# Attention and a gated product on one core: 128 partitions as two heads times 64 token groups, with the array used in tiles

## The chip, the cores and the metric

The kernel runs on one core of one Trainium2 chip. The metric is the device time of the launch in microseconds, lower is better. Times "before" are 292.38 and 290.5 us, median 291.44 us.

## The reference

For 8 batches and 8 heads of 576 tokens by 64 channels, q is put through a softmax over its channels, k through a softmax over the tokens. `kv` is the 64x64 product of the two token axes of k and v, and each token's output is its softmaxed q times `kv`. The result, as 4608 tokens by 512 channels (x), goes through a gated product and two matrices:

```
q_s = exp(q) / sum over channels         k_s = exp(k) / sum over tokens
kv = einsum('bhsd,bhse->bhde', k_s, v)   x = einsum('bhsd,bhde->bhse', q_s, kv)
a = x @ w1 ; b = x @ w2                  # w1, w2: 512 x 1024
out = ((a * b) @ w3) @ w_out             # w3: 1024 x 1024, w_out: 1024 x 512
```

The kernel folds w3 @ w_out into one 1024x512 matrix, W3O, once. All inputs and the output are float32, and the kernel computes in float16 with float32 sums.

## The kernel before, in words

One batch of 8 heads is the unit of the attention, one chunk of 512 tokens (of 9) the unit of what follows. A batch is 576 tokens, so chunk j needs batches up to j.

The attention of a batch has an elementwise part and a matrix part. A load (`load_qkv`) brings q, k or v of four heads; 96 partitions hold 6 tokens each (R = 6), so one row of a partition is 6 x 64 floats, 1536 bytes. `exp_k` and `exp_q` run on ScalarE (ACT) for a pair of heads at a time, `cast_v` on GpSimd (POOL) for four heads, and `norm_q` sums on VectorE (DVE), takes the reciprocal there, and multiplies on GpSimd. The matrix part is cut into pieces, which `pieces(b)` lists: `piece_t` transposes the normed q of a pair of heads (6 transposes into PSUM and one DVE copy to `qsT`), `piece_kv` accumulates `kv` of two pairs (12 matmuls; a column of 1/32 in v gives the sum of exp(k), so that DVE divides on the way to `kv2`), and `piece_x` multiplies `qsT` by a block-diagonal `kv2` (2 matmuls of 288 columns for a pair) and ScalarE copies the result into `xT`.

A chunk has 8 groups `s1` (four matmuls to `pa`, which ScalarE copies to float16; four to `pb`, which DVE multiplies with that copy) and, one chunk later, 4 groups `s2` (eight matmuls with W3O; DVE scales, and SyncE issues two stores of the rows). `w3_t` and `w3_m` make W3O: eight transposes of a row block of w3, then eight matmuls with w_out.

The order of the work is written out by hand: every engine runs its instructions in the order of the program. It is: loads and elementwise part of batch 0, its pieces, `s1` of chunk 0, the W3O loop (with the exps of the first half of batch 1 put in at `ft == 5`), then the four `s2` of chunk 0 between the pieces of batch 1, then the whole elementwise part of batch 2. From chunk 1 on, a table `seq` of 12 steps runs: each step has one `s1` or `s2`, then one piece of batch j+1, then one elementwise step of batch j+2, then perhaps a load of batch j+3. All loads and stores are issued by SyncE (SP), in program order. Every load goes into one of 9 slots of the pool `stage`, and waits until its slot is free. PSUM has three buffers for the attention (`pAtt`), three for `s1` (`pAB`) and two for `s2` and W3O (`pO`).

Of the kernel before, what the change touches and what calls it, by code (L numbers as in the profile page):

```python
# [16 lines left out]
def kernel(  # L17
# [11 lines left out]
    nc = tc.nc  # L29
# [4 lines left out]
    R = 6  # L34
    SP = S // R
    NPAIR = H // 2
# [9 lines left out]
    stage = ctx.enter_context(tc.tile_pool(name="stage", bufs=9))  # L46
    attn = ctx.enter_context(tc.tile_pool(name="attn", bufs=8))
# [4 lines left out]
    xT = [konst.tile([P, T], F16, name=f"xT{i}") for i in range(N_CT)]  # L52
    v16buf = [konst.tile([SP, H, R, 66], F16, name=f"v16_{i}") for i in range(2)]
    kv2buf = [konst.tile([P, 2, P], F16, name=f"kv2_{i}") for i in range(4)]
# [5 lines left out]
    def pAtt(shape, dtype):  # L60
        return psum.tile(shape, dtype, tag="att", name="att", bufs=3)
# [4 lines left out]
    def pO():  # L66
        return psum.tile([P, C], F32, tag="po", name="po", bufs=2)
# [7 lines left out]
    def load_qkv(b, which, hf):  # L75
        src = {"q": q, "k": k, "v": v}[which]
        t = slot([SP, 4, R * D])
        nc.sync.dma_start(  # L78
            out=t, in_=src[b, 4 * hf:4 * hf + 4].rearrange("h (p r) d -> p h (r d)", r=R))
        qkv32[(which, b, hf)] = t  # L80
# [22 lines left out]
    eks = {}  # L103
    eqs = {}
    eqns = {}

    def exp_k(b, p):
        t = qkv32[("k", b, p // 2)]
        ek = attn.tile([SP, R, 2, D], F16, tag="ek", name="ek", bufs=8)
        o = 2 * (p % 2)  # L110
        nc.scalar.activation(  # L111
            out=ek.rearrange("p r h d -> p h r d"),
            in_=t[:, o:o + 2].rearrange("p h (r d) -> p h r d", r=R), func=AF.Exp)
        eks[(b, p)] = ek

    def exp_q(b, p):
        t = qkv32[("q", b, p // 2)]
        eq = attn.tile([SP, R, 2, D], F16, tag="eq", name="eq", bufs=4)
        o = 2 * (p % 2)
        nc.scalar.activation(  # L120
            out=eq.rearrange("p r h d -> p h r d"),
            in_=t[:, o:o + 2].rearrange("p h (r d) -> p h r d", r=R), func=AF.Exp)
        eqs[(b, p)] = eq

    def cast_v(b, hf):
        t = qkv32[("v", b, hf)]
        nc.gpsimd.tensor_copy(  # L127
            out=v16buf[b % 2][:, 4 * hf:4 * hf + 4, :, 0:D],
            in_=t.rearrange("p h (r d) -> p h r d", r=R))

    def norm_q(b, p):
# [259 lines left out]
```

## Time and profile before

| | before |
|---|---|
| median of two runs | 291.44 us (290.5 and 292.38) |
| the profiled execution: time, span | 292.19 us, 290.4 us |
| mean granted TensorE clock | 0.964 |
| busy: PE, DVE, ACT, POOL | 245.5, 140.0, 124.3, 79.2 us |
| read and written in HBM | 38.80 MB, 9.44 MB |

The span runs from the first to the last instruction of the profiled execution; 1.8 us of its time lie outside the span. PE is TensorE's matmuls, PEld its weight loads, which run beside them. In rows of the timeline stand the start, the duration, the engine, the line of the kernel, the operation, what it writes and reads, shape and count, and in brackets the idle time before it and what ended that. A line with a form such as `96*128` names rows and columns of the array in use.

### The profile page before, as it was taken

What the parts mean: (1) busy time and instruction counts of PE and PEld (TensorE: products, weight loads), DVE (VectorE), ACT (ScalarE), POOL (GpSimd) and SP (SyncE); (2) the same over time, 40 slices, a digit from 0 to 9 for tenths busy, and PEclk for the clock granted to TensorE, in tenths of its full rate; (3) what the DMA queues carried; (4) which work ended last, traced back from release to release, by engine and by line L of the source; (5) the groups of instructions that cost most, each with busy time, mean ns of one, the idle gap of its engine ahead of it and who ended that gap; (6) DMA issues with size and microseconds to landing.
All of it is one profiled execution on the core that took longest, in us unless ns stands there. A gap on an engine that the chain in (4) does not pass through costs nothing.

```text
span 290.4 us, 3985 instructions
## 1 busy us (share of the span) xinstructions
PE 245.5 (85%) x1440; PEld 125.1 (43%) x1440; DVE 140.0 (48%) x268; ACT 124.3 (43%) x217; POOL 79.2 (27%) x64
## 2 busy tenths in 40 slices
PE   0218997739693399999999999999999999999993
PEld 0115444415441155555555455455555544444441
DVE  0344453231733468476476476657745434333441
ACT  3426542263344558556464456445622332121200
POOL 1461702305503456354125405505400000000000
PEclk9999999998888579999999999999999999999999
DMA  7999999990139999949946965971121112121124
GB/s 182 254 326 391 357 351 282 261 250 15 41 97 236 256 256 256 228 118 220 280 129 156 257 149 128 261 208 38 48 62 38 36 47 64 36 73 38 55 76 121
DMA packets 31443, 48.49 MB, mean 167 GB/s; under 512 B 2240, under 2 KB 24768, under 8 KB 31424
## 3 DMA queue, kind: packets, MB, share of 16 engines
q1 hardware_dynamic: 31424, 48.24, 62.3%
q8 instruction: 11, 0.18, 0.3%
q14 instruction: 8, 0.07, 0.1%
HBM read 38.80 MB, written 9.44 MB: 166 GB/s over the span
## 4 chain that ended last, share of the span: by engine, by line
PE 79%; DMA 8%; ACT 5%; DVE 3%; issue 1%; SPq 1%; DVEq 0%; ACTq 0%
PE pab L204 22%; PE pab L198 21%; PE po L215 21%; DMA st<-in_q_dram 8%; PE po L243 5%; PE att L152 4%; PE att L180 3%; PE att L169 2%; ACT eq L120 2%; ACT ek L111 1%; PE att L235 1%; DVE ds L134 1%; SPq L78 1%; DVE osb L218 0%; ACT w_542 L232 0%
## 5 line engine op out<-in xcount | busy, mean ns | idle before, releaser
L138 POOL TENSOR_TENSOR eqn<-eq,dr 96x768 f16<-96x768 f16 x32 | 46.8, 1470 | 98.9 <-DVE dr L136 57.5
L134 DVE TENSOR_REDUCE ds<-eq 96x12 f32<-96x768 f16 x32 | 30.0, 936 | 44.2 <-ACT eq L120 44.1
L215 PEld LDWEIGHTS <-abT 128*128 128x128 f16 x288 | 27.6, 99 | 30.5 <-issue 1.1
L218 DVE TENSOR_SCALAR osb<-po 128x512 f32<-128x512 f32 x36 | 24.8, 688 | 27.2 <-PE po L215 26.2
L120 ACT ACTIVATE eq<-st 96x768 f16<-96x768 f32 x32 | 26.4, 843 | 11.8 <-DMA st<-in_q_dram 11.8
L111 ACT ACTIVATE ek<-st 96x768 f16<-96x768 f32 x32 | 25.8, 843 | 8.5 <-DMA st<-in_k_dram 8.5
L169 PE MATMUL att<-ident,eqn 96*128 96x96 f16 x192 | 14.8, 219 | 7.7 <-POOL eqn L138 7.7
L152 PEld LDWEIGHTS <-ek 96*128 96x128 f16 x192 | 14.5, 108 | 13.9 <-ACT ek L111 7.0
L169 PEld LDWEIGHTS <-eqn 96*128 96x128 f16 x192 | 12.4, 105 | 13.9 <-POOL eqn L138 8.7
L152 PE MATMUL att<-v_0_75,ek 96*128 96x130 f16 x96 | 8.8, 254 | 10.0 <-POOL v_0_75 L127 10.0
L172 DVE COPY qsT<-att 128x576 f16<-128x576 f16 x32 | 14.2, 450 | 0.7 <-PE att L169 0.6
L204 PEld LDWEIGHTS <-w_0_85 128*128 128x128 f16 x72 | 7.4, 103 | 16.0 <-issue 8.6
L127 POOL CAST v_0_75<-st 96x1536 f16<-96x1536 f32 x8 | 11.7, 1461 | 9.2 <-DMA st<-in_v_dram 8.8
L215 PE MATMUL po<-W3O_93,abT 128*128 128x512 f16 x36 | 13.9, 386 | 0.0
L215 PE MATMUL po<-W3O_96,abT 128*128 128x512 f16 x36 | 13.9, 386 | 0.0
L215 PE MATMUL po<-W3O_95,abT 128*128 128x512 f16 x36 | 13.9, 385 | 0.0
L215 PE MATMUL po<-W3O_94,abT 128*128 128x512 f16 x36 | 13.9, 385 | 0.0
L215 PE MATMUL po<-W3O_97,abT 128*128 128x512 f16 x36 | 13.7, 381 | 0.0
L215 PE MATMUL po<-W3O_98,abT 128*128 128x512 f16 x36 | 13.6, 379 | 0.0
L215 PE MATMUL po<-W3O_99,abT 128*128 128x512 f16 x36 | 13.6, 379 | 0.0
L215 PE MATMUL po<-W3O_100,abT 128*128 128x512 f16 x36 | 13.6, 379 | 0.0
L204 PE MATMUL pab<-xT_71,w_0_85 128*128 128x512 f16 x18 | 7.3, 404 | 5.9 <-ACT a_880 L201 5.9
(265 smaller groups left out, 507.3 us busy)
## 6 DMA issues: line engine op xcount, KB each, us to landing
st<-in_k_dram SPq DMA_DIRECT2D x16, 576.0 KB, 9.7
st<-in_v_dram SPq DMA_DIRECT2D x16, 576.0 KB, 8.5
st<-in_q_dram SPq DMA_DIRECT2D x16, 576.0 KB, 10.0
st<-in_moe_w_dram SPq DMA_DIRECT2D x16, 512.0 KB, 7.7
out_dram<-osb SPq DMA_DIRECT2D x24, 192.0 KB, 2.3
out_dram<-osb SPq DMA_DIRECT2D x24, 128.0 KB, 2.3
st<-in_moe_w_out_dram SPq DMA_DIRECT2D x4, 512.0 KB, 5.5
out_dram<-osb SPq DMA_DIRECT2D x24, 64.0 KB, 2.0
```

The lines of the kernel that those rows point to most:

```text
L111: nc.scalar.activation(out=ek.rearrange("p r h d -> p h r d"), in_=t[:, o:o + 2].rearrange("p h (r d) -> p h r d", r=R), func=AF.Exp)
L120: nc.scalar.activation(out=eq.rearrange("p r h d -> p h r d"), in_=t[:, o:o + 2].rearrange("p h (r d) -> p h r d", r=R), func=AF.Exp)
L134: nc.vector.tensor_reduce(out=ds, in_=eq, axis=AX.X, op=ALU.add)
L138: nc.gpsimd.tensor_tensor(out=eqn.rearrange("p r h d -> p (r h) d"), in0=eq, in1=dr[:, :, None].broadcast_to([SP, 2 * R, D]), op=ALU.mult)
L152: nc.tensor.matmul(kvp[:, pp, :].rearrange("p (h e) -> p h e", h=2), lhsT=ek[:, r].rearrange("p h d -> p (h d)"), rhs=v16buf[b % 2][:, 2 * ...
L169: nc.tensor.transpose(pt[:, r, :], eqn[:, r].rearrange("p h d -> p (h d)"), ident[:SP, :SP])
L172: nc.vector.tensor_copy(out=qsT, in_=pt.rearrange("p r s -> p (r s)"))
L198: nc.tensor.matmul(pa, lhsT=w1sb[qt][:, ct, fo:fo + P], rhs=xT[ct][:, t0:t0 + CH], start=(ct == 0), stop=(ct == N_CT - 1))
L204: nc.tensor.matmul(pb, lhsT=w2sb[qt][:, ct, fo:fo + P], rhs=xT[ct][:, t0:t0 + CH], start=(ct == 0), stop=(ct == N_CT - 1))
L215: nc.tensor.matmul(po, lhsT=abT[(j, ft)][:, tb * P:(tb + 1) * P], rhs=W3O[ft], start=(ft == 0), stop=(ft == N_FT - 1))
L218: nc.vector.tensor_scalar(out=osb, in0=po, scalar1=ISC, scalar2=None, op0=ALU.mult)
L243: nc.tensor.matmul(wps, lhsT=w3Ts[ft][:, gt, :], rhs=wosb[gt // 2][:, gt % 2, :], start=(gt == 0), stop=(gt == N_FT - 1))
```

## The change

R becomes 9: a partition now holds 9 tokens of one head (2304 bytes in a row), 64 partitions hold a head, and 128 partitions hold two adjacent heads, g = 0 and 1. A load brings two such couples of heads (index hh), so it still covers four heads, and a half i of a batch is one such load of q, k and v. Elementwise instructions have 576 elements in each partition (one couple), or 1152 (two couples, in `norm_q`).

- `piece_kv(b, i)`: for each of 9 token rows two matmuls of 64 array rows, g = 0 and g = 1, into two PSUM banks; 18 matmuls, and two pieces in a batch.
- `piece_t(b, i)`: 9 transposes of 128x128 in place of 6 of 96x96; two in a batch, not four.
- `piece_x(b, i, hf)`: four matmuls of 64x64 array tiles (two row halves hh, two column halves g), 288 columns each; four pieces in a batch, and one ScalarE copy of 576 elements for each. `kv2` is no longer block-diagonal.
- `stage` has 12 slots, `pAtt` 2 buffers of two banks, `pO` one buffer; the last `s2` of the program and those of chunk 0 use `pAtt` in turn (`alt`).
- Order: q first in batch 0; w1 and w2 before w_out; two blocks of w3 ahead of w_out; all of w3 ahead of batch 1. Two `w3_t` stand within `s1` of chunk 0, and the W3O loop runs two blocks ahead. All casts of w3 are on GpSimd. Batch 1's exps begin after the seventh `w3_m`. The six loads of batch 2 are issued after the second `s2` of chunk 0, those of batch 3 after the fourth. In batch 0, v is cast by DVE and ACT, and the second half of q is multiplied by DVE.

```diff
-    R = 6
+    R = 9
-    stage = ctx.enter_context(tc.tile_pool(name="stage", bufs=9))
+    stage = ctx.enter_context(tc.tile_pool(name="stage", bufs=12))
...
+            in_=src[b, 4 * i:4 * i + 4].rearrange("(h g) (s r) d -> (g s) h (r d)", g=2, r=R))
...
+    def piece_kv(b, i):
+        kvp = pAtt([P, 2, 512], F32)
+        for r in range(R):
+            for g in range(2):
+                rows = slice(64 * g, 64 * g + 64)
+                nc.tensor.matmul(kvp[:, g, 0:130].rearrange("p (h e) -> p h e", h=2),
+                                 lhsT=eks[(b, i)][rows, r].rearrange("p h d -> p (h d)"),
+                                 rhs=v16buf[b % 2][rows, 2 * i:2 * i + 2, r, 0:65],
                                  start=(r == 0), stop=(r == R - 1))
...
+        for hh in range(2):
+            rows = slice(64 * hh, 64 * hh + 64)
+            for g in range(2):
+                nc.tensor.matmul(xp[64 * g:64 * g + 64, hh, 0:HS], lhsT=kv2[rows, g, :],
+                                 rhs=qsT[rows, g, cols], start=True, stop=True)
+        nc.scalar.copy(out=xT[:, 2 * i:2 * i + 2, b * S + hf * HS:b * S + (hf + 1) * HS],
+                       in_=xp[:, :, 0:HS])
...
-        (nc.scalar.copy if ft % 2 else nc.gpsimd.tensor_copy)(out=w316, in_=w32[("3", ft)])
+        nc.gpsimd.tensor_copy(out=w316, in_=w32[("3", ft)])
...
-        wps = pO()
+        wps = pO() if ft % 2 else pAB()
...
     for ft in range(N_FT):
-        if ft + 1 < N_FT:
-            w3_t(ft + 1)
         w3_m(ft)
-        if ft == 3:
-            for which in "kvq":
-                load_qkv(1, which, 1)
-        if ft == 5:
-            load_qkv(2, "k", 0)
-            elementwise(1, 0)
-    load_qkv(2, "v", 0)
-    load_qkv(2, "q", 0)
-    elementwise(1, 1)
+        if ft + 2 < N_FT:
+            w3_t(ft + 2)
+        if ft >= 6:
+            ew[2 * (ft - 6)]()
+            ew[2 * (ft - 6) + 1]()
...
+        s2(0, tb, alt=tb % 2)
+        ew[4 + tb]()
...
+        if tb == 1:
+            pc[1]()
+            for i in range(2):
+                load_qkv(2, "q", i)
+                load_qkv(2, "k", i)
+                load_qkv(2, "v", i)
```

Where the instructions moved, as the built programs have them. First ScalarE in the W3O loop, before; `w_` is a cast of a block of w3, `W3O` the copy of a finished block, `ek` and `eq` the exps of batch 1:

```order
L245 CAST W3O_96<-po 128x512
L232 CAST w_542<-st 128x1024
L245 CAST W3O_97<-po 128x512
L245 CAST W3O_98<-po 128x512
L111 ACTIVATE ek<-st 96x2x6x64 x2
L120 ACTIVATE eq<-st 96x2x6x64 x2
L232 CAST w_611<-st 128x1024
L245 CAST W3O_99<-po 128x512
```

And ScalarE at the same place now:

```order
L240 CAST W3O_91<-po 128x512
L240 CAST W3O_92<-pab 128x512
L114 ACTIVATE eq<-st 128x9x64 x2
L240 CAST W3O_93<-po 128x512
L107 ACTIVATE ek<-st 128x9x64 x2
L114 ACTIVATE eq<-st 128x9x64 x2
```

No cast of w3 stands on ScalarE any more, and no exp stands ahead of one. Second SyncE around the first stores, before; the three loads ahead of the stores are the first half of batch 2, those behind them its second half:

```order
L78 DMA st<-in_k_dram 96x4x384
L78 DMA st<-in_v_dram 96x4x384
L78 DMA st<-in_q_dram 96x4x384
L224 DMA out_dram<-osb 96x512
L224 DMA out_dram<-osb 32x512
L224 DMA out_dram<-osb 64x512 x2
L224 DMA out_dram<-osb 32x512
L224 DMA out_dram<-osb 96x512 x2
L224 DMA out_dram<-osb 32x512
L78 DMA st<-in_k_dram 96x4x384
```

And SyncE there now; the loads ahead of the stores are the second half of batch 1, the six between the stores are batch 2:

```order
L76 DMA st<-in_v_dram 128x2x576
L220 DMA out_dram<-osb 64x512 x4
L76 DMA st<-in_q_dram 128x2x576
L76 DMA st<-in_k_dram 128x2x576
L76 DMA st<-in_v_dram 128x2x576
L76 DMA st<-in_q_dram 128x2x576
L76 DMA st<-in_k_dram 128x2x576
L76 DMA st<-in_v_dram 128x2x576
L220 DMA out_dram<-osb 64x512 x4
```

Of batch 2, no load stands ahead of the stores now; all six stand behind four of the eight.

More of the change, by code (lines that the diff above doesn't have):

```diff
@@ L100, in load_w3 @@
         w32[("3", ft)] = t
[L103 to L123, printed above, removed]
@@ L245, in w3_m @@
         nc.scalar.copy(out=W3O[ft], in_=wps)
[L248 to L257 removed]
+    ctx.enter_context(tc.manual_schedule())
+    acopy, vcopy, pcopy = nc.scalar.copy, nc.vector.tensor_copy, nc.gpsimd.tensor_copy
+    for i in range(2):
+        for which in "qkv":
+            load_qkv(0, which, i)
     load_w12(0, 0)
```

288 lines of the change are left out of this document (150 added, 138 removed).

## The prediction

> **What bounds the kernel now.** I read the page's 40 slices first. A slice is 7.26 us; each digit is a busy share in tenths.
>
> ```profile
> span 290.4 us, 3985 instructions
> PE   0218997739693399999999999999999999999993
> DMA  7999999990139999949946965971121112121124
> ```
>
> From the fifteenth slice (about 102 us) on, PE is full to the last slice but one. All idle time that a change of order could take away lies before it, and there the DMA row is full until 65 us. So there are two questions: how much earlier the full stretch starts, and whether a chunk in it gets shorter. For the first I read the timeline of PE and ACT at each gap:
>
> ```profile
> 6.09 1.58 ACT L111 ACTIVATE ek<-st 96x768 f16<-96x768 f32 x2 [4.06 <-DMA st<-in_k_dram]
> 8.46 1.46 POOL L127 CAST v_0_75<-st 96x1536 f16<-96x1536 f32 x1 [6.67 <-DMA st<-in_v_dram]
> 9.97 1.46 PE L152 MATMUL att<-v_0_75,ek 96*128 96x130 f16 x12 [9.97 <-POOL v_0_75 L127]
> 10.75 1.58 ACT L120 ACTIVATE eq<-st 96x768 f16<-96x768 f32 x2 [3.08 <-DMA st<-in_q_dram]
> 27.21 0.63 PE L198 MATMUL pab<-xT_71,w_0_81 128*128 128x512 f16 x1
> 42.58 0.61 PE L235 MATMUL att<-ident,w_431 128*128 128x128 f16 x8
> 49.89 0.62 PE L235 MATMUL att<-ident,w_490 128*128 128x128 f16 x8 [1.62 <-ACT w_490 L232]
> 65.10 1.03 PE L235 MATMUL att<-ident,w_611 128*128 128x128 f16 x8 [4.55 <-ACT w_611 L232]
> 70.36 0.38 PE L215 MATMUL po<-W3O_93,abT 128*128 128x512 f16 x1
> 85.48 0.38 PE L198 MATMUL pab<-xT_71,w_0_81 128*128 128x512 f16 x1
> 97.20 1.58 ACT L120 ACTIVATE eq<-st 96x768 f16<-96x768 f32 x2 [3.07 <-DMA st<-in_q_dram]
> 99.29 0.58 PE L204 MATMUL pab<-xT_71,w_0_85 128*128 128x512 f16 x1 [5.88 <-ACT a_880 L201]
> ```
>
> These rows cut the start into five stages: batch 0's attention until 27.21, `s1` of chunk 0 until 42.58, the W3O loop until 70.36, batch 1 with `s2` of chunk 0 until 85.48, and a stall in the second group of chunk 1 until 99.29. In the third, PE waits for casts of w3 on ACT; the longest wait, 4.55 us, is for the cast that stands behind batch 1's exps. In the fifth, the copy `a_880` stands on ACT behind batch 2's exps, and those wait for loads.
>
> For the second question, the fourth `s2` of three chunks in the chain of waits:
>
> ```profile
> 211.64 1.73 PE po L215 x8
> 235.78 1.73 PE po L215 x8
> 256.50 1.73 PE po L215 x8
> ```
>
> A chunk with a batch's pieces takes 24.14 us (211.64 to 235.78), one without 20.72: the pieces cost PE 3.42 us a batch, on the path, six times (batches 2 to 7).
>
> **The loads.** The windows show what the loads get (the last two columns are DMA share and GB/s):
>
> ```profile
> 4.00:17.70 13.70, 2.78 (x24) 2.19 (x24) 2.21 (x4) 4.74 (x7) 5.77 (x4) 1.00 1.08 252
> 17.70:40.00 22.30, 17.47 (x85) 8.61 (x86) 11.98 (x24) 11.56 (x20) 8.30 (x7) 1.00 1.01 362
> 88.00:106.00 18.00, 8.74 (x42) 4.45 (x43) 8.11 (x16) 8.12 (x12) 8.67 (x6) 0.62 1.06 256
> ```
>
> The first and the third are loads of q, k and v into 96 partitions, the second is weights into 128; the engines are full in all. One load of 589.8 KB at 252 takes 2.33 us, at 362 it takes 1.63. The new load is 128 partitions with rows of 2304 bytes. I take 1.63, since the row with 128 partitions is the nearest, and keep 2.33 as the other end. The Trainium skill ("SBUF — State Buffer", Door 1: the DMA port swizzle) has 16 ports of 8 partitions, by which 96 partitions fill half of the ports only half; it would give 252/0.75 = 336 GB/s, an estimate, 1.76 us a load and about 1 us on the sum below.
>
> **The elementwise work** shrinks by a quarter per batch, since 128 partitions share it. Groups that I scale by elements:
>
> ```profile
> L138 POOL TENSOR_TENSOR eqn<-eq,dr 96x768 f16<-96x768 f16 x32 | 46.8, 1470 | 98.9 <-DVE dr L136 57.5 <-ACT xT_71 L182 37.1 <-PE pab L198 2.6
> L134 DVE TENSOR_REDUCE ds<-eq 96x12 f32<-96x768 f16 x32 | 30.0, 936 | 44.2 <-ACT eq L120 44.1
> L120 ACT ACTIVATE eq<-st 96x768 f16<-96x768 f32 x32 | 26.4, 843 | 11.8 <-DMA st<-in_q_dram 11.8
> L232 POOL CAST w_467<-st 128x1024 f16<-128x1024 f32 x1 | 1.0, 1043 | 7.5 <-PE att L235 7.5
> L201 ACT CAST a_346<-pab 128x512 f16<-128x512 f32 x1 | 0.6, 586 | 1.1 <-PE pab L198 1.1
> L161 DVE TENSOR_TENSOR kv_0_77<-att,rc 64x128 f16<-64x128 f32 x8 | 2.3, 289 | 0.2
> L172 DVE COPY qsT<-att 128x576 f16<-128x576 f16 x32 | 14.2, 450 | 0.7 <-PE att L169 0.6
> L237 DVE COPY w3T<-att 128x1024 f16<-128x1024 f16 x8 | 5.5, 690 | 11.6 <-PE att L235 11.6
> ```
>
> An exp of 576 elements: 843 x 0.75, about 0.65 us. A sum: 0.70. A multiply of 1152 on POOL: 1.5 x 1.47 = 2.2. A copy of 1152 to `qsT`: by 450 at 576 and 690 at 1024, 0.76. A copy of x, 576 elements on ACT: by 586 at 512, 0.65. The division after `kv`: two of 0.29 and the reciprocal, about 0.75. In the full stretch PE is the bound and not these engines, so the quarter is worth nothing there; in the first stages it shortens the chain.
>
> **The stages.** *Batch 0.* Before, k's first exp starts at 6.09 and q's, two loads later, at 10.75, so a load takes 2.33 and the first began near 3.8. With 1.63 each and q first, the first lands near 5.4, the rest at 7.0, 8.7, 10.3, 11.9, 13.5. The chain then is DVE's: v cast until 9.5 (0.4 an instruction, by the 690 for 1024), nine passes of two `kv` matmuls to 10.6 (0.12 a pass, by the 12 in 1.46 at this place, where PE is slower than later), division, transposes to 11.7, `qsT` to 12.5, the two sums of the second half to 13.9, reciprocal and its multiply on DVE (1.2 ns an element, by the sum's 936 for 768) to 15.5, transposes to 16.6, `kv` to 17.7, division to 18.5, two x pieces and two copies to 20.2. Before: 27.21. Gain 7.0.
>
> *`s1` of chunk 0* takes 15.4 before (27.21 to 42.58) and gets two `w3_t` of 0.45 more: loss 0.9, end at 36.5. Its weights land in time: six loads to 13.5, then eight of 524 KB at 1.45 to 25.1; two of w3 and four of w_out by 33.8, and the last of the four is cast near 36.
>
> *W3O loop.* The cost of its parts, two rows of the timeline back to back and one of the chain of waits:
>
> ```profile
> 45.93 0.61 PE L235 MATMUL att<-ident,w_467 128*128 128x128 f16 x8
> 46.38 0.59 PE L243 MATMUL po<-wo_89,w3T 128*128 128x512 f16 x2
> 46.54 1.74 PE po L243 x8
> ```
>
> Eight transposes take 46.38 - 45.93 = 0.45 us, eight matmuls 1.74. Now 8 x 1.74 + 6 x 0.45 = 16.6, in place of 27.8 (42.58 to 70.36), if nothing waits: the casts are on POOL (1.04 us each, one for each 2.19 us), run two blocks ahead, and the last block of w3 lands near 42.5, while its transposes stand near 49. Gain 11.2; end at 53.1. If a wait of one cast stayed in every second block, as the 1.62 us above, it would be 6 less.
>
> *Batch 1 and `s2` of chunk 0.* Before 15.1 (70.36 to 85.48). Now four `s2` of 1.73 with a wait of 1.5 in them for the first multiply on POOL (exps from 51.8, two sums and the reciprocal to 54.1, multiply to 56.3), and 1.2 of pieces between them, end at 62.7. Behind the fourth, with two `pAtt` buffers, the rest goes in turn: transposes, scaling and copy to `qsT` (0.69 and 0.76), `kv` 0.53, division 0.75, two x pieces and copies 1.5, with the transposes 4.8. End at 67.5: gain 0.7. The loads of batch 2 stand on SP behind four stores, which need the second `s2`, finished near 58.6; they are issued near 60 and land from 64.8 on (4.6 after the issue, by the first load above with 1.63), the fifth (the last k) near 71.3.
>
> *The stall.* ACT has eight exps of 0.65 from 67.5, until 72.7 with no load late; then `a16` of the first group to 73.3, and the second group's `pb` goes on near 74.3. Before, the same instruction started at 99.29, 13.8 after the first `s1`; now 6.8 after. Gain 7.0. DMA is about 1 us from being late here.
>
> Sum of the five: 7.0 - 0.9 + 11.2 + 0.7 + 7.0 = 25.0 us earlier. I summed without hand-overs; one takes 0.05 (the v cast ends at 9.92, the matmul that waits starts at 9.97), some thirty in these chains, 1.5. So 23.5. Batch 3's loads follow behind batch 2's, every 1.63 us, ahead of their exps at a step of 2 us each.
>
> **The pieces in the full stretch.** What one takes now, from start to the start of the next kind:
>
> ```profile
> 142.50 0.42 PE L169 MATMUL att<-ident,eqn 96*128 96x96 f16 x6
> 142.75 0.38 PE L198 MATMUL pab<-xT_71,w_0_81 128*128 128x512 f16 x1
> 144.48 0.86 PE L152 MATMUL att<-v_0_75,ek 96*128 96x130 f16 x12
> 145.19 0.38 PE L215 MATMUL po<-W3O_93,abT 128*128 128x512 f16 x1
> 145.41 0.38 PE L215 MATMUL po<-W3O_94,abT 128*128 128x512 f16 x1
> 82.35 0.41 PE L180 MATMUL att<-qsT,kv_2_79 128*128 128x288 f16 x2
> 82.60 0.42 PE L169 MATMUL att<-ident,eqn 96*128 96x96 f16 x6
> ```
>
> Transposes of 96 columns are 42 ns each, matmuls of 130 columns 59, of 288 columns 125: 24 x 42 + 24 x 59 + 8 x 125 = 3.42 us, which is the difference of the chunks. Now 18 transposes of 128 columns (0.45/8 = 56 ns) are 1.01. The 36 `kv` matmuls are 18 x 59 = 1.06 if the two row halves run at once, 36 x 59 = 2.12 if not. The 16 matmuls of x are 4 x 125 = 0.50 if four tiles run at once, 2.0 if not. So 2.57 or 5.13 a batch, -0.85 or +1.71.
>
> No row of before shows the array changing its tiling. The nearest is the tail of a matmul that does not wait for the one before: a 512-column matmul has a record of 0.38 us and the next starts 0.216 later (145.19, 145.41), so up to 0.164 could show each time the array has to empty. A batch has two `kv` pieces and four x pieces between others: 12 changes, at most 2.0 us; at least nothing, if the next weights come in meanwhile. I take half, 0.98, with overlapping tiles: 2.57 + 0.98 = 3.55, +0.13 a batch, +0.8 in all. The Trainium skill ("TensorEngine Tiling (Array Packing)", Key Properties) says that a change of tiling mode drains the array, and that tiles run independently; by that the whole tail is paid, and that is the first rival.
>
> **Sum.** 292.2 (the profiled execution, 0.75 above the median) - 23.5 + 0.8 = 269.5. I write 270.
>
> **The rivals.** *Every change empties the array, tiles overlap.* 2.57 + 1.97 = 4.54 a batch, +1.12, six times 6.7: 275.4. For it: six pieces in a batch stand between full-size work. Against: no row; weight loads run ahead now (PEld beside PE).
>
> *Loads stay at 252 GB/s.* The bound is then the row size or HBM and not the partitions. Batch 0 loses 2 (its last v lands at 17.7), the W3O loop 1 (w_out lands 4 later), the stall 3 (the fifth load 9.3 after the first, not 6.5), batch 3's first exp 2: 8 in all, 277. Against: at 1 KB rows the weights had 362.
>
> *The start gives less.* The stall in chunk 1 stays as long as before (of batch 2, nothing is issued ahead of the stores now): 7 less, 276.5.
>
> *Tiles take turns, changes are cheap.* +1.71 seven times (batch 1 too) is 12.0, and batch 0's chain, with twice the `kv` passes at 0.12 (2.2) and x in turns (1.5), 3.7: 284.4, at the edge of what 2% can tell.
>
> *Slower: tiles take turns and every change also shows a weight load.* 5.13 + 12 x (0.164 + 0.10) = 8.30 a batch, +4.9; seven batches 34.2, batch 0 3.7: 292.2 - 23.5 + 37.9 = 306.6. The change turns against itself from (23.5 - 3.7)/7 = 2.8 us more a batch on, 6.2 in place of 3.42. The 0.10 is a weight load, as this row has it:
>
> ```profile
> L215 PEld LDWEIGHTS <-abT 128*128 128x128 f16 x288 | 27.6, 99 | 30.5 <-issue 1.1
> ```
>
> For it: 70 weight loads a batch in place of 56, on half-size tiles. Against: the 96-column transposes already go at 42 ns each with one load per matmul.
>
> **How the numbers follow.** Chances: forecast 0.45 (its own range 264, no cost of changes, to 275); every change empties 0.18; loads slow 0.10; start gives less 0.11; take turns 0.10; slower 0.06. The range 261 to 285 holds the first five nearly whole; its low end lets the start come 2.5 us earlier than summed. Two runs of before differ by 0.6%, so 2% is what can be told from no change: below 285.6 is faster. The first four are, and half of the fifth; with two in a hundred off for mishaps, faster 0.87, same 0.07, slower 0.06.
>
> **What would show it.** `s1` of chunk 0 starts near 20 to 21 and the W3O loop near 37; no wait on a cast of w3; the second group of chunk 1 goes on near 75; loads of q, k, v run at 360 GB/s. In the full stretch the fourth `s2` of two chunks stand 24.3 apart: 23.3 means free changes, 25.3 the drained array, 25.9 and more tiles that take turns. I would be wrong if that distance passes 27, or if PE's full stretch still starts after 90.

## The result and the profile after

The changed kernel takes 272.8 us (median of 272.52 and 273.09), before 291.44: a ratio of 0.936, with a 95% interval of 0.922 to 0.950. Run once more beside other versions it took 271.75 us, ratio 0.932 (0.928 to 0.936). The profiled execution took 272.52 us, its span is 270.7. The forecast for it was 269.5, so the sum was 3.0 us short.

The page of the kernel after, its 40 slices of 6.77 us each:

```profile
span 270.7 us, 4110 instructions
PE   0459999986779999999999999999999999999982
DMA  7999999118999604883495469212211113112235
```

PE is now busy from the fourth slice on, with one dip to 6 and 7 tenths in slices ten to twelve, where before it came down to 3 tenths in three slices and was full only from the fifteenth on. The DMA row is no longer full to the end of the start: it has two holes, at 47 to 61 us and at 95 to 102.

The timeline of the kernel after, at the ends of the five stages and at what they wait for:

```profile
4.49 1.26 ACT L114 ACTIVATE eq<-st 128x576 f16<-128x576 f32 x2 [2.48 <-DMA st<-in_q_dram]
19.63 2.00 PE L197 MATMUL pab<-xT,w_0_74 128*128 128x512 f16 x4
24.95 1.06 PE L203 MATMUL pab<-xT,w_0_78 128*128 128x512 f16 x4
37.11 0.59 PE L238 MATMUL pab<-wo_82,w3T 128*128 128x512 f16 x2
54.44 0.38 PE L214 MATMUL po<-W3O_86,abT 128*128 128x512 f16 x1 [0.67 <-ACT W3O_93 L240]
63.00 0.75 DVE L127 TENSOR_REDUCE ds<-eq 128x9 f32<-128x576 f16 x1
66.38 0.68 PE L165 MATMUL att<-ident,eqn 128*128 128x128 f16 x9 [2.06 <-POOL eqn L134]
70.22 2.11 PE L197 MATMUL pab<-xT,w_0_74 128*128 128x512 f16 x4
73.82 2.12 POOL L134 TENSOR_TENSOR eqn<-eq,dr 128x1152 f16<-128x1152 f16 x1 [6.28 <-DVE dr L132]
75.99 0.98 PE L165 MATMUL att<-ident,eqn 128*128 128x128 f16 x9 [2.50 <-POOL eqn L134]
76.76 1.91 PE L197 MATMUL pab<-xT,w_0_74 128*128 128x512 f16 x4
78.47 1.06 PE L203 MATMUL pab<-xT,w_0_78 128*128 128x512 f16 x2
```

The stages of the sum, in us: before and after from the starts of these instructions, the forecast from its own terms, where 75.8 is the forecast's 74.3 with the 1.5 of hand-overs put in, and 191.9 is the 191.1 of before with the 0.8 of the pieces:

| | before | forecast | after |
|---|---|---|---|
| batch 0's attention, until `s1` starts | 27.21 | 20.2 | 19.63 |
| `s1` of chunk 0 | 15.37 | 16.3 | 17.48 |
| W3O loop | 27.78 | 16.6 | 17.33 |
| batch 1 and `s2` of chunk 0 | 15.12 | 14.4 | 15.78 |
| stall, until `pb` of the second group | 13.81 | 6.8 | 8.25 |
| hand-overs, charged in one sum | | 1.5 | in the stages |
| `pb` of the second group starts at | 99.29 | 75.8 | 78.47 |
| from there to the end of the span | 191.1 | 191.9 | 192.2 |

So the start became 20.8 us shorter and the rest 1.1 us longer. The gain is batch 0 (7.6), the W3O loop (10.45) and the stall (5.6); the two stages between them became longer by 2.1 and 0.7.

The kernel after was profiled once more in its later run (270.29 us, span 268.5). In the order of the table its stages are 19.72, 16.03, 17.33, 16.25, 7.15 and 192.0. So two executions of one kernel differ by up to 1.5 us in a stage: by 1.45 in `s1` of chunk 0, 0.5 in batch 1 and 1.1 in the stall. A difference of that size between forecast and measurement says nothing about the change to the kernel.

Two windows of the kernel after, the first loads and `s1` of chunk 0; the last three columns are the granted clock, the DMA share and GB/s:

```profile
3.00:13.00 10.00, 2.62 (x35) 2.11 (x35) 5.01 (x10) 3.77 (x6) 2.12 (x1) 1.00 1.02 373
19.63:37.11 17.48, 17.48 (x81) 7.59 (x82) 7.78 (x12) 9.30 (x14) 8.52 (x8) 1.00 1.05 388
```

The loads have 373 GB/s with engines as full as they were at 252. The lengths that the forecast had scaled from the smaller tiles hold: the multiply on POOL was put at 2.2 us and is 2.12, the sum at 0.70 and is 0.75 (the rows at 73.82 and 63.00 above).

The chain of waits after, the fourth `s2` of the same three chunks:

```profile
190.38 1.73 PE po L214 x8
214.98 1.73 PE po L214 x8
235.70 1.73 PE po L214 x8
```

A chunk with pieces now takes 24.60 us, before 24.14; one without, 20.72 as before. The pieces cost PE 3.88 us a batch and not 3.42. The timeline of PE around one piece of `kv` and one of x in the full stretch shows of what these consist:

```profile
145.83 1.03 PE L203 MATMUL pab<-xT,w_0_78 128*128 128x512 f16 x4
146.79 0.69 PE L148 MATMUL att<-v_1_73,ek 64*128 64x130 f16 x18
147.42 0.39 PE L214 MATMUL po<-W3O_86,abT 128*128 128x512 f16 x1
149.15 0.67 PE L165 MATMUL att<-ident,eqn 128*128 128x128 f16 x9
149.66 1.03 PE L197 MATMUL pab<-xT,w_1_75 128*128 128x512 f16 x4
150.52 1.03 PE L203 MATMUL pab<-xT,w_1_79 128*128 128x512 f16 x4
151.48 0.32 PE L179 MATMUL att<-qsT,kv_1749 64*64 64x288 f16 x4
151.72 1.04 PE L197 MATMUL pab<-xT,w_1_75 128*128 128x512 f16 x4
```

Four matmuls of 512 columns take 0.86 from start to start (149.66 to 150.52). What follows the four at 145.83 comes after 0.96, and so it does at 150.52: 0.10 us lie in front of each piece in a new tiling. The 18 `kv` matmuls take 0.63, the four of x 0.24, the nine transposes 0.51, which are in full-size tiling. With two, four and two pieces: 2 x 0.73 + 4 x 0.34 + 2 x 0.51 = 3.84, against the 3.88 of the chunks. Overlapping tiles without a price for changes would be 2.57, as forecast; the 1.3 above it are twelve changes of 0.11. Six of them are the gaps in front of the pieces; the other six, back to full-size tiling, lie within the 0.63 and the 0.24.

### The profile page after: what moved, and what is told of

Its sections match the earlier page's. It is cut to its first block, busy times and chain, and to the rows that moved or that the text cites. A ratio compares the mean times of both kernels' runs of the same rounds, so it can differ in the third digit from the quotient of the medians.

```text
span 270.7 us, 4110 instructions
## 1 busy us (share of the span) xinstructions
PE 244.1 (90%) x1552; PEld 114.0 (42%) x1552; DVE 134.3 (50%) x236; ACT 108.1 (40%) x182; POOL 62.6 (23%) x63
## 4 chain that ended last, share of the span: by engine, by line
PE 87%; DVE 5%; POOL 2%; DMA 2%; ACT 1%; issue 1%; SPq 0%; POOLq 0%; DVEq 0%; ACTq 0%
PE pab L197 24%; PE pab L203 23%; PE po L214 20%; PE att L148 4%; PE att L165 4%; PE att L179 3%; PE pab L238 3%; POOL eqn L134 2%; DMA st<-in_v_dram 2%; PE att L214 2%; PE po L238 2%; DVE ds L127 2%; PE att L230 1%; DVE osb L217 1%; ACT xT L181 1%
## 5 line engine op out<-in xcount | busy, mean ns | idle before, releaser
L134 POOL TENSOR_TENSOR eqn<-eq,dr 128x1152 f16<-128x1152 f16 x15 | 31.8, 2121 | 99.7 <-PE att L179 48.6
L181 ACT CAST xT<-att 128x576 f16<-128x576 f32 x32 | 20.1, 639 | 37.4 <-PE att L179 37.4
L127 DVE TENSOR_REDUCE ds<-eq 128x9 f32<-128x576 f16 x32 | 23.6, 750 | 10.7 <-ACT eq L114 10.3
L114 ACT ACTIVATE eq<-st 128x576 f16<-128x576 f32 x32 | 21.3, 685 | 5.9 <-DMA st<-in_q_dram 5.9
L197 PE MATMUL pab<-xT,w_0_74 128*128 128x512 f16 x72 | 22.2, 433 | 0.1
L107 ACT ACTIVATE ek<-st 128x576 f16<-128x576 f32 x32 | 21.3, 682 | 0.2 <-DMA st<-in_k_dram 0.2
L203 PE MATMUL pab<-xT,w_0_78 128*128 128x512 f16 x72 | 20.3, 408 | 0.0
L165 PE MATMUL att<-ident,eqn 128*128 128x128 f16 x144 | 11.9, 234 | 8.1 <-POOL eqn L134 5.6
L197 PE MATMUL pab<-xT,w_2_76 128*128 128x512 f16 x72 | 18.6, 381 | 0.0
L197 PE MATMUL pab<-xT,w_1_75 128*128 128x512 f16 x72 | 18.5, 380 | 0.0
L197 PE MATMUL pab<-xT,w_3_77 128*128 128x512 f16 x72 | 18.5, 379 | 0.0
L203 PE MATMUL pab<-xT,w_2_80 128*128 128x512 f16 x72 | 18.5, 379 | 0.0
L203 PE MATMUL pab<-xT,w_3_81 128*128 128x512 f16 x72 | 18.5, 379 | 0.0
L203 PE MATMUL pab<-xT,w_1_79 128*128 128x512 f16 x72 | 18.5, 379 | 0.0
L165 PEld LDWEIGHTS <-eqn 128*128 128x128 f16 x144 | 9.9, 105 | 12.7 <-POOL eqn L134 7.1
L168 DVE COPY qsT<-att 128x1152 f16<-128x1152 f16 x16 | 12.0, 751 | 4.0 <-PE att L165 3.9
L214 PE MATMUL po<-W3O_86,abT 128*128 128x512 f16 x32 | 12.3, 384 | 1.5 <-DVE osb L217 0.8
## 6 DMA issues: line engine op xcount, KB each, us to landing
st<-in_moe_w_out_dram SPq DMA_DIRECT2D x4, 512.0 KB, 11.2
```

The costliest lines, as they stand in the source:

```text
L107: nc.scalar.activation(out=eks[(b, i)][:, :, hh, :], in_=qkv32[("k", b, i)][:, hh].rearrange("p (r d) -> p r d", r=R), func=AF.Exp)
L114: nc.scalar.activation(out=eqs[(b, i)][:, :, hh, :], in_=qkv32[("q", b, i)][:, hh].rearrange("p (r d) -> p r d", r=R), func=AF.Exp)
L127: nc.vector.tensor_reduce(out=dss[(b, i)][:, :, hh], in_=eqs[(b, i)][:, :, hh, :], axis=AX.X, op=ALU.add)
L134: eng.tensor_tensor(out=eqn.rearrange("p r h d -> p (r h) d"), in0=eqs[(b, i)].rearrange("p r h d -> p (r h) d"), in1=dr[:, :, None].broad ...
L165: nc.tensor.transpose(pt[:, r, :], eqns[(b, i)][:, r].rearrange("p h d -> p (h d)"), ident)
L181: nc.scalar.copy(out=xT[:, 2 * i:2 * i + 2, b * S + hf * HS:b * S + (hf + 1) * HS], in_=xp[:, :, 0:HS])
```

## The experiments

The theory was: tiles of different halves run at once and a change of tiling costs about half a tail (it is nearer to two thirds, as seen above); the loads are faster because they reach 128 partitions; the start is shorter because w3's casts left ScalarE and because of the shorter elementwise chain. The rivals were the ones of the prediction. Every version was run beside the kernel before on the same chip; ratios are to that one.

**The `kv` halves one after the other.** If they run at once, issuing one half's nine matmuls before the other's takes that away.

```diff
-        for r in range(R):
-            for g in range(2):
+        for g in range(2):
+            for r in range(R):
```

> The kv matmuls of the changed kernel in another order: all nine of the upper 64 rows, then all nine of the lower, in place of turn by turn. Theory (the two row halves run at once): a kv piece grows from 0.63 us to about 1.06 (18 x 59 ns), a full chunk from 24.60 to about 25.5, the whole from 272.8 to about 278 to 280. Rival (halves take turns anyway, and a 64-row matmul is simply shorter): piece 0.63, chunk 24.60, time 272.8.

Measured: 277.73 us, ratio 0.951 (0.946 to 0.956), about 5 us longer than with the halves in turn and a little under the 278 to 280 expected. The timeline of PE and the chain of waits of this version:

```profile
150.29 1.00 PE L148 MATMUL att<-v,ek 64*128 64x130 f16 x18
151.22 1.90 PE L214 MATMUL po<-W3O,abT 128*128 128x512 f16 x8
```

```profile
169.88 1.73 PE po L214 x8
195.09 1.73 PE po L214 x8
```

The same 18 matmuls take 0.93 us in place of 0.63, 52 ns each in place of 35, and the chunk 25.21 in place of 24.60 (0.61, which is two pieces of 0.30). Both times hold one change back, about 0.1 us; without it they are some 29 and 46 ns each, an estimate, and 29 is half of the 59 of before. So two row halves do run at once, and wholly only where the instructions of the two halves alternate. The rival that tiles take turns is out: in turns without overlap the 18 are 1.06 by the 59 ns of the prediction, and their order would not matter. What takes the time in the order half by half (the loading of weights or the matmuls themselves) no run here separates.

**x pieces in pairs.** Two pieces of x follow each other, so that the array changes 8 times a batch and not 12; nothing else is added or left out.

```diff
-                lambda: piece_x(b, 0, 0), lambda: piece_kv(b, 1), lambda: piece_x(b, 0, 1),
-                lambda: piece_x(b, 1, 0), lambda: piece_x(b, 1, 1)]
+                lambda: (piece_x(b, 0, 0), piece_x(b, 0, 1)), lambda: piece_kv(b, 1), lambda: None,
+                lambda: (piece_x(b, 1, 0), piece_x(b, 1, 1)), lambda: None]
```

> The two x pieces of a half batch stand directly behind each other in the changed kernel, so a batch has 8 changes of tiling in place of 12; the work is the same. Theory (each change costs about 0.11 us, tiles overlap): full chunk 24.60 to about 24.15, whole 272.8 to about 270. Rival (no price for a change; an x piece takes 0.24 us since its four tiles take turns in part): chunk stays at 24.5 to 24.6, time 272 to 273.

Measured: 269.66 us, ratio 0.925 (0.920 to 0.930). The chain of waits of this version:

```profile
163.67 1.73 PE po L214 x8
187.80 1.73 PE po L214 x8
```

The chunk is 24.13 us, 0.47 less for four changes, 0.118 each: the price that the gaps showed above, now as a difference. It is more than nothing and less than the 0.164 of a whole tail. The timeline of PE of this version also settles whether the four tiles of x overlap:

```profile
149.83 0.44 PE L179 MATMUL att<-qsT,kv 64*64 64x288 f16 x8
150.20 1.04 PE L197 MATMUL pab<-xT,w 128*128 128x512 f16 x4
```

Eight matmuls of x take 0.37 us and four took 0.24, so the second four add 0.13, as much as one full-size matmul of 288 columns (0.125 in the prediction): the four tiles run at once.

**The new order in the old layout.** The tiles of 96 partitions, with the new order of loads and of w3, the casts on GpSimd, the loop two blocks ahead, and batch 1's elementwise work later. `stage` keeps its 9 slots, the PSUM buffers are those of before, and the casts and the multiply that the change puts on other engines in batch 0 stay where they were. Only a part of the edit is shown.

```diff
-        (nc.scalar.copy if ft % 2 else nc.gpsimd.tensor_copy)(out=w316, in_=w32[("3", ft)])
+        nc.gpsimd.tensor_copy(out=w316, in_=w32[("3", ft)])
...
-        for which in "kvq":
+        for which in "qkv":
...
-        if ft + 1 < N_FT:
-            w3_t(ft + 1)
         w3_m(ft)
-        if ft == 5:
-            load_qkv(2, "k", 0)
+        if ft + 2 < N_FT:
+            w3_t(ft + 2)
+        if ft == 6:
             elementwise(1, 0)
```

> The old layout (96 partitions, 6 tokens, full-size matmuls, block-diagonal kv2, 9 load slots) with the new order: q first, w1 and w2 before w3 and w_out, w3 ahead of batch 1, two W3O transposes within s1, loop two blocks ahead, casts of w3 on GpSimd, batch 1's exps behind the seventh W3O block, batch 2's loads behind the second s2. Theory (the order gives the W3O loop's 10.5 us, the layout the rest through faster loads): W3O loop about 17.5 us, s1 of chunk 0 near 27, second group of chunk 1 goes on near 88 to 89, chunk 24.14, whole about 279 to 282. Rival (the layout gives nearly all, since loads bind everywhere): 287 or more. Rival (the order gives all): 273 or less.

Measured: 284.1 us, ratio 0.972 (0.965 to 0.979): later than expected, and between the two kernels. A window of its first loads and the timeline of PE:

```profile
3.00:17.00 14.00, 2.42 (x24) 2.41 (x25) 5.25 (x12) 6.30 (x8) 6.14 (x5) 1.00 1.07 258
```

```profile
24.51 1.91 PE L198 MATMUL pab<-xT,w 128*128 128x512 f16 x4
75.69 1.21 PE L198 MATMUL pab<-xT,w 128*128 128x512 f16 x4
87.70 0.59 PE L204 MATMUL pab<-xT,w 128*128 128x512 f16 x1 [5.15 <-ACT a L201]
```

The order alone is worth 7.3 us, and what the change has besides it (the layout, the slots and buffers, the engines in batch 0) about 11.3, the rest of the 18.6. The W3O loop takes 19.0 us there (41.18 to 60.19) and waits for no cast, so most of that stage's gain is the order's. With the old tiles the loads stay at 258 GB/s, `s1` starts at 24.51 (4.9 later than with both), and the stall in chunk 1 is still 12.0 us (75.69 to 87.70), with a wait of 5.15 for the copy behind batch 2's exps. The chain of waits runs through batch 2's loads there:

```profile
72.01 9.93 DMA st<-in_q_dram
```

So of the 5.6 us that the stall lost the order gives 1.8, and the rest comes with the layout: the faster loads and the larger tiles, as far as argued. Whether the 9 slots have a part in it wasn't tried.

**Rows of half the size.** Every load of q, k and v is split into two DMAs with rows of 1152 bytes, less than the 1536 of before, still into 128 partitions.

```diff
-        nc.sync.dma_start(
-            out=t,
-            in_=src[b, 4 * i:4 * i + 4].rearrange("(h g) (s r) d -> (g s) h (r d)", g=2, r=R))
+        rows = src[b, 4 * i:4 * i + 4].rearrange("(h g) (s r) d -> (g s) h (r d)", g=2, r=R)
+        for n in range(2):
+            part = slice(n * R * D // 2, (n + 1) * R * D // 2)
+            nc.sync.dma_start(out=t[:, :, part], in_=rows[:, :, part])
```

> Each load of q, k and v in the changed kernel split into two with rows of 1152 bytes, still 128 partitions. Theory (the 96 partitions held the old loads to 252 GB/s): the loads of batch 0 run at 340 to 375 GB/s as with rows of 2304 bytes, time within 2 us of 272.8. Rival (the row size did): the loads fall to about 250 GB/s or less, batch 0 ends 2 us or more later, whole 276 or more.

Measured, in a single run: 271.06 us. The window of its first loads:

```profile
3.00:13.00 10.00, 2.23 (x27) 1.92 (x28) 4.31 (x9) 4.94 (x7) 2.12 (x1) 1.00 1.07 350
```

350 GB/s with rows shorter than those that had 252 and 258: the row size was not the bound. Of the differences between the loads that were looked at, the number of partitions is the one left.

**Batch 1's elementwise work earlier.** Between the W3O loop and chunk 1 PE waits 0.67 us for the copy of the last block (its buffer is the only one of `pO`, which the first `s2` needs), and 1.06 and 2.06 for the two multiplies of batch 1. (Two more waits, 0.70 and 0.58, lie within the chain of batch 1's last pieces.) Here batch 1's steps begin after the fourth block of the loop and not the seventh, and the last block goes to `pAB`.

```diff
-        wps = pO() if ft % 2 else pAB()
+        wps = pAB() if ft % 2 else pO()
...
-        if ft >= 6:
-            ew[2 * (ft - 6)]()
-            ew[2 * (ft - 6) + 1]()
+        for f in {3: (0,), 4: (1,), 5: (2,), 6: (3, 4), 7: (5, 6)}.get(ft, ()):
+            ew[f]()
```

> In the changed kernel, batch 1's elementwise steps begin after the fourth W3O block in place of the seventh, and the last W3O block goes into a pAB buffer, so that pO is free for the first s2. Theory (batch 1's three PE waits of 0.67, 1.06 and 2.06 us are on the path, and its loads are in by 47 us): they go, the rest of the kernel moves up by 3 to 4.5 us, to about 268.5 to 270. Rival (behind them the copies to qsT and the loads of batch 2 end late too): 272 or more.

Measured: 267.29 us, ratio 0.915 (0.909 to 0.922). About 5 us are gained, and the three waits are gone. The timeline of PE and ACT of this version shows what is late next:

```profile
69.11 1.26 ACT L114 ACTIVATE eq<-st 128x576 f16<-128x576 f32 x2 [0.80 <-DMA st<-in_q_dram]
70.74 0.88 PE L165 MATMUL att<-ident,eqn 128*128 128x128 f16 x9 [3.22 <-POOL eqn L134]
```

Chunk 1 starts 5.4 us earlier (64.85 against 70.22; two matmuls later it waits 0.61 for `xT`). The three waits are 3.8 of that; 0.8 is that `s1` of chunk 0 was at full pace earlier in this execution (16.6 against 17.48). But the wait for the first multiply of batch 2 grows from 2.50 to 3.22, and an exp now waits for its load.

**Groups of chunk 1 between the exps of batch 2.** If the copy on ScalarE behind the eight exps is what holds up the second group, two groups put between the exps should pass.

```diff
-    for f in ew:
+    for f in ew[0:3]:
+        f()
+    s1(1, 0)
+    ew[3]()
+    s1(1, 1)
+    for f in ew[4:]:
         f()
```

> In the changed kernel the first two s1 of chunk 1 are put between the exps of batch 2 (after the third and the fourth elementwise step) in place of behind them all. Theory (the stall of 76 us is ACT's order: the copy of the first s1 stands behind eight exps): both groups are done near 76 in place of 80, whole about 269 to 270.5. Rival (the stall is the wait for batch 2's loads, issued behind the stores): the exps end no earlier and the next pieces wait in their place, 272 or more.

Measured: 273.96 us, ratio 0.938 (0.932 to 0.944), no gain at all; the theory's time failed. The timeline of PE and POOL of this version:

```profile
76.31 0.67 PE L165 MATMUL att<-ident,eqn 128*128 128x128 f16 x9
79.11 2.12 POOL L134 TENSOR_TENSOR eqn<-eq,dr 128x1152 f16<-128x1152 f16 x1 [2.14 <-DVE dr L132]
81.29 0.68 PE L165 MATMUL att<-ident,eqn 128*128 128x128 f16 x9 [3.57 <-POOL eqn L134]
```

The two groups pass as thought: the transposes behind them start at 76.31. But the exps, sums and the multiply of the second half move back behind them, and its transposes wait 3.57 us. The wait has moved. With the copy out of the way the chain of the elementwise work of batch 2 bounds the stall as before, so that the place of the copy alone is not its cause.

**Batch 2's loads ahead of the stores.** The rival that the start gives less because these loads stand behind four stores.

```diff
     pc = pieces(1)
+    for i in range(2):
+        for which in "qkv":
+            load_qkv(2, which, i)
     for tb in range(4):
         s2(0, tb, alt=tb % 2)
```

> In the changed kernel batch 2's six loads are issued ahead of the first stores, directly behind batch 1's. Theory (the stall in chunk 1 is ACT's exps, which find their loads in): time within 1 us of 272.8. Rival of the prediction (the stall is set by loads that stand behind stores): 268 or less.

Measured: 271.78 us, ratio 0.930 (0.923 to 0.936), not to be told from the kernel after. The timeline of ACT and PE of this version:

```profile
70.72 1.27 ACT L114 ACTIVATE eq<-st 128x576 f16<-128x576 f32 x2
75.56 1.14 PE L165 MATMUL att<-ident,eqn 128*128 128x128 f16 x9 [1.96 <-POOL eqn L134]
```

The exps stand back to back until 75.3, none waits for a load, and the transposes still wait for the multiply. That rival is out for this kernel.

**Every second cast of w3 on ScalarE again.** This is one line of the change undone.

```diff
-        nc.gpsimd.tensor_copy(out=w316, in_=w32[("3", ft)])
+        (nc.scalar.copy if ft % 2 else nc.gpsimd.tensor_copy)(out=w316, in_=w32[("3", ft)])
```

> In the changed kernel every second cast of w3 goes back to ScalarE; the loop still transposes two blocks ahead. Theory (the old loop's wait of 1.62 us in every second block came from the cast standing on ScalarE behind the copy of a W3O block): three such waits come back, W3O loop 17.3 to about 22, whole about 277 to 278. Rival (transposing two blocks ahead is what removed them): loop 17.3, 272.8.

Measured: 278.36 us, ratio 0.954 (0.945 to 0.962). The timeline of PE in the loop:

```profile
42.77 0.62 PE L230 MATMUL att<-ident,w 128*128 128x128 f16 x8 [1.62 <-ACT w L227]
```

Three waits of 1.62 us are back (the others, at 48.91 and 55.05, are not shown), as long as the one shown of before, although the casts are issued two blocks ahead, and one of 0.76 stands within `s1`. The cast stands on ScalarE behind the copy of a finished block, and so waits for the matmuls it should run ahead of. In before, the blocks cast on GpSimd were not waited for at a distance of one block (the row at 45.93 in the prediction). Not the distance but the engine was the cause.

**A better version, in three steps.** First the edits of x in pairs, batch 1 earlier, and loads ahead of the stores together.

```diff
-                lambda: piece_x(b, 1, 0), lambda: piece_x(b, 1, 1)]
+                lambda: (piece_x(b, 1, 0), piece_x(b, 1, 1)), lambda: None]
...
+        for f in {3: (0,), 4: (1,), 5: (2,), 6: (3, 4), 7: (5, 6)}.get(ft, ()):
+            ew[f]()
     pc = pieces(1)
+    for i in range(2):
+        for which in "qkv":
+            load_qkv(2, which, i)
```

> The x pieces in pairs, batch 1's elementwise steps early, and batch 2's loads ahead of the stores, all three on the changed kernel. Theory (three separate places on the path: tiling changes, batch 1's waits, and loads that come late once batch 1 is early): -3.1, -5.2 and -1 to -2 from 272.8, so 262.5 to 264.5. Rival (the start is bound by one thing, so the second and third overlap): 266 or more.

Measured: 265.65 us, ratio 0.911 (0.907 to 0.914), between the 262.5 to 264.5 of the theory and the 266 of the rival. The timeline of PE:

```profile
70.59 1.14 PE L165 MATMUL att<-ident,eqn 128*128 128x128 f16 x9 [3.21 <-POOL eqn L134]
75.06 0.68 PE L165 MATMUL att<-ident,eqn 128*128 128x128 f16 x9
```

With the loads earlier the transposes of batch 2 still come at 70.59 after a wait of 3.21 (70.74 and 3.22 with batch 1 earlier alone): the loads give nothing here either. Without their 1 to 2 us the sum would have been 264.5. Whether the other two gains overlap in the 1.1 us that are left can't be told: the changed kernel itself differs by as much between two sets of runs (272.8 and 271.75). Next the first multiply of batch 2 goes from GpSimd to VectorE:

```diff
-    ew = elementwise_steps(2)
+    ew = elementwise_steps(2, nc.vector)
```

> The kernel of the three edits, and the first multiply of batch 2 on VectorE in place of GpSimd (1.36 against 2.12 us). Theory (in the stall of chunk 1, PE's transposes wait for that multiply): 0.7 to 1.5 less than with three edits. Rival (ACT's exps set it alone): the same within 0.5.

Measured: 264.26 us, ratio 0.907 (0.904 to 0.909), 1.4 us less than the version before; the two intervals overlap. The timeline of PE:

```profile
71.12 0.68 PE L165 MATMUL att<-ident,eqn 128*128 128x128 f16 x9 [2.34 <-DVE eqn L134]
75.08 0.68 PE L165 MATMUL att<-ident,eqn 128*128 128x128 f16 x9 [0.93 <-POOL eqn L134]
```

The wait is 0.87 us shorter. The transposes come 0.5 later than in the version before, but they and the matmuls behind them go at full pace (the nine in 0.68 and not 1.14). Then the transposes of the second half wait 0.93 for their multiply, which is still on GpSimd, and start at 75.08, where the version before had them at 75.06. The two profiled executions are also alike as a whole (264.31 and 264.42 us). So these traces don't show where the 1.4 us between the medians come from, and that the shorter wait gave them is not shown. Last, from batch 3 on both `kv` pieces follow each other, which leaves six changes a batch:

```diff
+        if b > 2:
+            return [lambda: piece_t(b, 0), lambda: None, lambda: piece_t(b, 1), lambda: None,
+                    lambda: (piece_kv(b, 0), piece_kv(b, 1)), lambda: None,
+                    lambda: (piece_x(b, 0, 0), piece_x(b, 0, 1)), lambda: None,
+                    lambda: (piece_x(b, 1, 0), piece_x(b, 1, 1))]
```

> The same, and from batch 3 on the two kv pieces directly behind each other, so 6 changes of tiling a batch in place of 8. Theory (0.11 a change): a full chunk 24.14 to about 23.9, five chunks, 1.1 less. Rival (each buffer of pAtt is now wanted sooner, so PE waits for the copies): chunk 24.1 or more.

Measured: 262.53 us, ratio 0.901 (0.897 to 0.904), the fastest version of all. In its chain of waits:

```profile
133.28 1.73 PE po L219 x8
157.21 1.73 PE po L219 x8
```

The chunk is 23.93 us, 0.20 less than with eight changes (24.13) for two changes: 0.10 each, the same price a third time. Five chunks make 1.0 of the 1.7 us by which this version is faster.

Beside these three the changed kernel ran again, unchanged, as the measure for them.

> The changed kernel itself, on the same chip as the three before: 272.5 to 273.1 by its earlier runs; if the chip differs, the differences above are read against this one.

Measured: 271.75 us, ratio 0.932 (0.928 to 0.936). The three edits give 6.1 us beyond it, all five 9.2.

## Why the prediction was right

The time lies in the range, the direction is right, and of the cases it was the likeliest one. Step by step:

- *Batch 0, 7.0 us shorter forecast, 7.6 measured.* Right. The first load's exp starts at 4.49 and not near 5.4, which is more than the difference.
- *`s1` of chunk 0, 0.9 longer forecast, 2.1 measured.* The step "gets two `w3_t` of 0.45 more" is right (the transposes are there). It took the pace of PE to be as before, and in this execution PE ran slowly for longer. In the timeline after, the matmuls start 0.42 us apart until 24.95, 5.3 us after the stage began; in before the same pace lasted 3.1, as these rows of its timeline show:

```profile
28.92 0.63 PE L204 MATMUL pab<-xT_71,w_0_85 128*128 128x512 f16 x1
...
30.49 0.38 PE L198 MATMUL pab<-xT_71,w_0_81 128*128 128x512 f16 x1
```

  Of 2.2 us more at half the pace, half is lost: 1.1 of the 1.2 missed. But the second profiled execution of the same kernel is at full pace by 22.77, 3.05 us after its stage began at 19.72, and its W3O loop starts at 35.75; there the stage is 16.03 long, near the 16.3 of the forecast. Two rows of PE of that execution, the second for the stall below:

```profile
35.75 1.89 PE L238 MATMUL pab<-wo,w3T 128*128 128x512 f16 x8
75.10 0.68 PE L165 MATMUL att<-ident,eqn 128*128 128x128 f16 x9 [1.95 <-POOL eqn L134]
```

  So this miss comes and goes with the execution and is not the change's.
- *W3O loop, 11.2 shorter forecast, 10.45 measured.* The matmuls and transposes of the loop take 16.66, as summed; the wait of 0.67 for the copy of the last block ahead of the first `s2` was not in the sum. That no cast is waited for, and why, the run with the casts back on ScalarE showed.
- *Batch 1 and `s2`, 0.7 shorter forecast, 0.7 longer measured (1.1 in the second execution).* The step that failed is "behind the fourth ... the rest goes in turn". The transposes of the second half don't come in turn: they wait 2.06 for their multiply on GpSimd. Its sum is at 63.00 on VectorE, behind the scalings of the `s2`, and the multiply at 64.20. I had given one wait, for the first multiply, 1.5 us; it is 1.06, and the second was missing. Moving the elementwise work forward took these waits and the 0.67 away and gave about 5 us.
- *The stall, 7.0 shorter forecast, 5.6 measured.* The cause that I named, "ACT has eight exps ..., then `a16`, and `pb` goes on", is only one of two things that are late together. ScalarE is as forecast (exps of 71.16 to 75.75, the copy thereafter). But on PE the transposes of batch 2 stand ahead of the second group, and these wait until 75.99 for the multiply on GpSimd, which began at 73.82; then `pa` comes first, at half pace (1.71), and `pb` at 78.47. So the chain is exp, sum, reciprocal, multiply, transposes, and the run with groups between the exps, which went round the copy, gained nothing. In the second execution the transposes wait as well (1.95, until 75.10), but they and `pa` go at full pace and the stall is 7.15, near the 6.8 of the forecast: most of the 1.45 missed is pace, which differs between executions, and the cause named is incomplete all the same.
- *Hand-overs, 1.5 longer forecast.* They lie within the stages and can't be read apart; with them the start was missed by 2.7 us (0.7 in the second execution).
- *The pieces, 0.13 a batch longer forecast, 0.46 measured.* The term that was too small is the change of tiling. Overlap of the tiles was right (35 ns a matmul of `kv`, 52 where the halves don't alternate, and 0.13 us for the second four tiles of x). A change was put at 0.082 and is 0.10 to 0.12. Over six chunks this makes +2.8 and not +0.8; but from the second group on the whole is only 1.1 longer. PE leaves its slow phase at about 80 us, right after the stall, where before it went on to 105; that can make up the difference, though it was not worked out to the tenth. The forecast had no such term, and that the two errors cancel was luck.

The Trainium skill ("TensorEngine Tiling (Array Packing)", Key Properties) says that a change of mode drains the array. The gaps agree in that a change is not free: 0.11 us. By a full tail of 0.164 the chunk would have been 25.3 us, and it is 24.60. So the price of that rival was too high; whether what is paid is a drain, no run here shows.

*The rivals.* Loads at 252 GB/s: out, by 373 and by the run with half rows (350). Start held up by the stores: out, by the run with the loads ahead of them. Tiles in turns, and with it the slower case: out, by 0.63 us for 18 matmuls, which become 0.93 when the halves stand apart. That every change empties the array at the price of a whole tail: out, as a change costs two thirds of it.

## What to carry to other kernels

Tiles that are smaller than the array run at once if their instructions alternate, and pieces of the same shape should stand together, since each change costs about 0.11 us; here four changes fewer gave 0.47 us a chunk. The tiling itself did not gain PE anything in the kernel after: the pieces of a batch cost 3.88 us with twelve changes, 3.41 with eight and 3.21 with six, against 3.42 before. What paid was the layout that it allows, with its faster loads and its shorter elementwise chain, and the order. A cast or copy that is meant to run ahead must not stand on an engine behind a copy that waits for the work it feeds (1.62 us in every second block). When a stall has two causes that end at almost the same time, taking one away moves the wait to the other: read the chain of the work that was put ahead, too, before the price is put down to one instruction.

## What the runs showed of the hardware that was not expected

Two tiles of 64 rows run wholly at once only if issued in alternation: 35 ns a matmul of 130 columns in turn, 52 ns one half after the other (each with its share of the change back), 59 ns in full-height tiling before (96 rows). A change between this tiling and the full one costs 0.10 to 0.12 us.

A load of the same 590 KB runs at 252 and 258 GB/s into 96 partitions and at 373 into 128, with the engines full in all; with rows of half the size at 350. By the 16 ports of 8 partitions of the Trainium skill ("SBUF — State Buffer", Door 1: the DMA port swizzle) the ratio would be 0.75, an estimate; the measured 252/373 is 0.68 and 258/350 is 0.74, so the ports would explain most of it.

PE's slow phase, in which matmuls of 512 columns start 0.43 us apart and not 0.22, lasted 5.3 us at the first `s1` after, 3.1 before, and at most 3.05 in the second execution of the kernel after; the granted clock of these windows reads 1.00 all the same. In the stall of chunk 1 the granted clock does show it: it reads 0.50 from 70 to 72 us in the first execution.

The length of a pause does not decide whether the slow phase comes back. After a pause of 3.21 us PE went at half pace (nine transposes in 1.14) and after one of 2.34 at full pace (0.68), but after one of 3.57 the transposes went at full pace too (0.68, with the groups between the exps) and half pace came only about 1 us later. And after a pause of 1.95, with half pace ahead of it, PE went at full pace in the second execution (0.68), while after one of 1.96, with half pace ahead of it as well, it went at half pace with the loads ahead of the stores (1.14). The Trainium skill ("TensorE: Matmul & The Clock Gate", Part 1) has a free-running window of about 3.4 us, of idling before the array slows and of work before it recovers. A window that runs free would fit the different lengths in one kernel. That an idle window must come first does not fit: in the kernel after, the granted clock reads 1.00 from 66 to 68 us and 0.50 from 70 to 72, and the pauses ahead of that were 2.06, 0.70 and 0.58 us. What decided it, no run here shows.
